# Kernel tables of a state-space layer formed by half chunks of 64 channels instead of quarters of 32

## The chip, the cores and the metric

The kernel runs on one core of a Trainium2 chip. The core has a matrix engine (TensorE, PE in the profile), a vector engine (VectorE, DVE), an engine for functions and casts (ScalarE, ACT), a general engine (GpSimd, POOL) and an engine that mostly issues transfers (SyncE, SP). Each engine runs its instructions in the order in which they stand in its own stream and waits where an operand or a buffer is not ready. The metric is the time of one execution on the device, in microseconds.

## The reference

Two independent layers read their own inputs, and their outputs stand side by side in the result. Part A is attention in which each position sees eight earlier positions, two apart. Part B is a state-space convolution with 640 channels, 192 complex states per channel and 2048 positions:

```python
a: qkv = x @ wqkv                                   # 2048 x 640, 32 heads of 20
   logits = q . k[pos - 2 w] * 20**-0.5, w = 0..7;  attn = softmax;  out = (attn . v) @ wo
b: logdA = dt * (A_re + 1j * A_im)                  # 640 x 192
   P = jnp.exp(logdA[:, :, None] * l[None, None, :])
   K = jnp.einsum("dn,dnl,dn->dl", Cc, P, dB).real  # 640 x 2048, sum over the 192 states
   y = irfft2(rfft2(u, padded) * rfft2(K, padded))[:L] + u * Dskip
```

Nearly all that this document speaks of belongs to K, the sum over 192 states at 2048 positions for 640 channels, and to the Fourier transforms behind it.

## The kernel before, in words

**Chunks, halves, quarters.** The 640 channels are done in five chunks (`NCH = 5`, index `c`) of 128 channels. A chunk has two halves of 64 channels (index `h`), and a half has two quarters of 32 (index `uu`). States lie on partitions. Of a quarter's 32 channels the first 128 states fill all 128 partitions in 32 columns, one a channel; the last 64 states fill 64 partitions, so two channels share each of 16 more columns. The 48 columns are 12 groups `q` of 4 (`f`), and for the sum over states there are matmuls on 128 rows and matmuls on 64.

**Tables.** A power exp(logdA * l) is split into a product of a factor for l's low six bits and one for the rest. The magnitudes come from ACT exponentials (`exps_chunk`, L230 and L232, 45 a chunk, tile `R`). The angles are formed by matmuls into the PSUM tiles `ps_ph` (L257, L260) and turned into sines by ACT (`trig_half`, L264): four tiles `TA` and four tiles `TX` a half. `ps_ph` comes from the pool that also serves the Fourier transforms (tag `bank2`, three buffers).

**Products on DVE.** `small_half` (L280 in the profile, where its helper `TT` is) multiplies the tables of one half: `PG` = magnitude times sine, `Q` = PG times the coefficients `cT`, sums of these into `F` and `G` (both in the tile PG), and per quarter a tile `X` in three operations. `y_form` (L310) then forms, per quarter and for each of k = 0, 1, 2, a tile `Y` from F and G: 12 groups of 64 positions of 4 columns, 3072 elements a partition. Y has the tag `Y` with four buffers, and Q takes one of them.

**Kernel sums on TensorE.** `kgen_unit` (L323 and L328) runs, per quarter and k, 32 matmuls on all 128 partitions and then 32 on 64 partitions, all into one PSUM bank `ps_k` (two buffers). ACT copies that bank into `Ksb` (L329) once a quarter.

**The rest of a chunk.** `coefficients` (L211) makes `cT` for the next chunk by TensorE and four ACT copies. `fwd` transforms (matmuls and casts `A` at L342, L343, then `Sg` at L348, L349), once for K (`transform`) and once for the input u (`fwd_u`). `products` multiplies the two spectra on DVE (`P1`, `P2`, L363). `inverse_a` is the first stage of the inverse transform (matmuls L379, casts `Z` L380). `times_d` (L392) forms the products `UD` of u with the skip weights.

**Order.** The loop over chunks at the end of the program emits, for chunk c: the half-0 products, the transform of chunk c-1, the tables of half 1, the quarter units of half 0 with `products` and `inverse_a` of chunk c-1 between them, `fwd_u`, the half-1 products, the next chunk's coefficients, exponentials and half-0 tables, and the quarter units of half 1. A scheduler then sets each engine's stream by its own estimates; `keep_in_program_order` and `issue_after` pin some instructions to places in it. After the loop stand attention and the second stage of the inverse transform. From 0 to 31 us the program prepares, from 31 to about 298 us it is in the chunk loop, from there to the end in attention and the rest.

Of the kernel before, what the change touches and what calls it, by code (L numbers as in the profile page):

```python
# [10 lines left out]
A = mybir.AluOpType  # L11
# [3 lines left out]
f32 = mybir.dt.float32  # L15
# [79 lines left out]
def partB_prep(tc, pools, prm):  # L95
# [108 lines left out]
    def coefficients(c, pool):  # L204
        for u in range(4):
            sl = slice(32 * u, 32 * u + 32)
            ps = pool.tile([128, 4, UW], f32, name="ps_tr", tag="bank")
            re, im = CN[sl, c, 0], CN[sl, c, 1]
            transposed(u, [(ps[:, 0:4], re, mix[sl, 0:4], True), (ps[:, 1:4], im, mix[sl, 4:7], False),
                           (ps[:, 3:4], re, mix[sl, 7:8], False), (ps[:, 2:3], im, mix[sl, 8:9], False)])  # L210
            nc.scalar.copy(out=cT[:, c, u // 2, :, 12 * (u % 2):12 * (u % 2) + 12, :].rearrange("p w q f -> p w (q f)"), in_=ps[:])  # L211

# [60 lines left out]
def small_half(tc, pools, co, R, TA, TX, h):  # L273

    nc = tc.nc
    V = nc.vector
    tab = pools["tabb"]
    RA, RX = R
    RX = RX[:, 24 * h:24 * h + 24].rearrange("p q (j i) f -> p q j (i f)", j=2)
    TT = lambda o, a, b, op: V.tensor_tensor(out=o, in0=a, in1=b, op=op)  # L280
# [10 lines left out]
    Xs = []  # L291
    for uu in range(2):
        qs = slice(12 * uu, 12 * uu + 12)
        X = tab.tile([128, 12, 3, 32, 4], bf16, name="X", tag="X", bufs=2)
        rows = X[:].rearrange("p q k (j i) f -> p q (k j) (i f)", j=2)
        T = TX[:, qs].rearrange("p q s i f -> p q s (i f)")
        TT(rows[:, :, 0:2], RX[:, qs], bc(T[:, :, 0], 2, 2), A.mult)
        TT(rows[:, :, 2:6:3], RX[:, qs], bc(T[:, :, 1], 2, 2), A.mult)
        TT(rows[:, :, 4:2:-1], rows[:, :, 0:2], rows[:, :, 2:6:3], A.subtract)
        Xs.append(X)  # L300
    return F, G, Xs


def y_form(tc, pools, F, G, uu, k):
    nc = tc.nc
    Y = pools["tabb"].tile([128, 12, 64, 4], bf16, name="Y", tag="Y", bufs=4)
    half = slice(384 * uu, 384 * uu + 384)
    fa = F[:, k, half].rearrange("p (q a f) -> p q a f", a=8, f=4).unsqueeze(2).to_broadcast([128, 12, 8, 8, 4])
    gb = G[:, k, half].rearrange("p (q b f) -> p q b f", b=8, f=4).unsqueeze(3).to_broadcast([128, 12, 8, 8, 4])
    nc.vector.tensor_tensor(out=Y[:].rearrange("p q (b a) f -> p q b a f", a=8), in0=fa, in1=gb, op=A.mult)  # L310
    return Y


def kgen_unit(tc, pools, u, X, Ys, Ksb):

    nc = tc.nc
    MM = nc.tensor.matmul
    ps = pools["psum"].tile([128, 8, 64], f32, name="ps_k", tag="bank", bufs=2)
    for k in range(3):
        for t in range(8):  # L320
            for g in range(4):
                q, f = divmod(8 * g + t, 4)
                MM(ps[32 * g:32 * g + 32, t], lhsT=X[:, q, k, :, f], rhs=Ys[k][:, q, :, f], start=(t == 0 and k == 0), stop=False, tile_position=(0, 32 * g), skip_group_check=True)  # L323
        for t in range(8):
            for g in range(4):
                q, f = divmod(32 + 8 * (g % 2) + t, 4)
                hb = slice(64 * (g // 2), 64 * (g // 2) + 64)
                MM(ps[32 * g:32 * g + 32, t], lhsT=X[hb, q, k, :, f], rhs=Ys[k][hb, q, :, f], start=False, stop=(k == 2), tile_position=(64 * (g // 2), 32 * g), skip_group_check=True)  # L328
    nc.scalar.copy(out=Ksb[:, 8 * u:8 * u + 8, :], in_=ps[:])  # L329

# [77 lines left out]
class Attention:  # L408
# [3 lines left out]

    def __init__(self, tc, pools, A_x, A_wqkv, A_wo, out_a, psk, psg):
# [4 lines left out]
        self.one = lambda name: psg.tile([128, 512], f32, name=name, tag="bank", bufs=2)  # L418
# [39 lines left out]
    def open_first(self, tabb):  # L458

        tile = lambda n, tag, **k: tabb.tile([128, n, 4, 256], bf16, name="prod0", tag=tag, **k)  # L460
        U, K, Y, P = tile(1, "UD"), tile(2, "Ksb"), tile(3, "Y", bufs=4), tile(4, "PG")
        self.first = [[U[:, 0], K[:, 0], Y[:, 0], P[:, 0], P[:, 2]], [Y[:, 2], K[:, 1], Y[:, 1], P[:, 1], P[:, 3]]]
# [229 lines left out]
def body(tc, ctx, pools, prm, B_u, B_Dskip, Sd, Zd, UDd, A_x, A_wqkv, A_wo, out_a, out_b):  # L692
# [14 lines left out]
    with tc.tile_pool(name="prep_l", bufs=1) as pl, tc.tile_pool(name="prep_d", bufs=1) as pd, tc.tile_pool(name="prep_g", bufs=1) as pg, tc.tile_pool(name="prep_h", bufs=1) as ph, tc.tile_pool(name="psum_p", bufs=2, space=bass.MemoryType.PSUM) as psp:  # L707
# [3 lines left out]
        fill(0, 1, lambda u: None)  # L711
        B["coefficients"](0, psp)
        Dn = pl.tile([128, 160], bf16, name="Dn")
# [11 lines left out]
        nc.gpsimd.tensor_copy(out=Dsb[:], in_=Dn[:].rearrange("p (ut c) -> p c ut", c=NCH))  # L725
    psg = ctx.enter_context(tc.tile_pool(name="psum_g", bufs=2, space=bass.MemoryType.PSUM))
    pools["tabb"] = tabs.enter_context(tc.tile_pool(name="tabb", bufs=1, reuse_waits="tile"))
    pools["tabb"].tile([128, LOW], bf16, name="low")
    att = Attention(tc, pools, A_x, A_wqkv, A_wo, out_a, psk, psg)
    Kb, Sk = {}, {}  # L730

    def transform(c):
        Sk[c] = fwd(tc, pools, C, (lambda ut: Kb[c][:, ut, :]), 1, fp)[0]

    def unit(c, h, uu, F, G, X, between=lambda: None):
        Ys = [y_form(tc, pools, F, G, uu, k) for k in range(3)]
        between()
        kgen_unit(tc, dict(pools, psum=psg), 2 * h + uu, X, Ys, Kb[c])
        if 4 * c + 2 * h + uu in UD_AFTER:
            times_d(tc, pools, C, UDd, *divmod(UD_AFTER.index(4 * c + 2 * h + uu), 2))  # L740

# [6 lines left out]

    UD_AFTER = [2, 3, 5, 6, 7, 9, 10, 11, 13, 14]
    LAST = NCH - 1  # L750
    for c in range(NCH):
        Kb[c] = (fp, pools["tabb"])[c % 2].tile([128, 32, 64], bf16, name="Ksb", tag="Ksb")
        F, G, Xs = small_half(tc, pools, B["cT"][:, c], R[c], *trig[c, 0][:2], 0)
# [21 lines left out]
        with ExitStack() as order:  # L775
            if c > 0:
                order.enter_context(tc.issue_after(last.ins))
            F, G, Xs = small_half(tc, pools, B["cT"][:, c], R[c], *trig[c, 1][:2], 1)
# [171 lines left out]
```

## Time and profile before

| | before |
|---|---|
| median of 3 runs | 436.23 us (433.06, 436.23, 437.49) |
| the profiled execution | 432.86 us |
| its span, first to last instruction | 431.1 us |
| mean granted TensorE clock | 0.945 |
| DVE, PE, ACT busy | 379.2, 365.2, 314.1 us |
| Y (60 instructions) | 103.1 us busy, 5.0 us idle ahead of them |
| PG, X waiting for ACT's tables | 7.4 and 3.7 us |
| copies of ps_k (20) | 11.5 us busy, 12.8 us idle ahead of them |

A group's line in the profile reads: line of the program, engine, operation, output <- inputs with partitions and elements per partition, number of instructions, then total busy us and mean ns of one, then the us that the engine stood idle just ahead of these instructions and what ended most of that. Line numbers are those of the program above. A row of 40 digits shows the busy share of each fortieth of the span in tenths. In the timeline a row gives the start in us, the time that a run of equal instructions took, and in brackets the idle time before it.

### The profile page before, as it was taken

To read this page: it belongs to the slowest core of one execution; us is meant where nothing else is said; L and a number is where in the kernel's file an instruction comes from. 1 tells how busy PE (TensorE), PEld (TensorE's weight loads), DVE (VectorE), ACT (ScalarE), POOL (GpSimd) and SP (SyncE) were. 2 spreads that over 40 slices of the span, in tenths; PEclk is the share of its full clock that TensorE was granted. 3 is DMA by queue.
4 is the path that set the end of the run, shared out by engine and by line. 5 is a ranking of instruction groups with operands and counts; after the bars stand their busy time and mean duration, and the time that the engine had idled before them with its cause. 6 is when DMAs were issued, how large, how long until landed. Compare 5 with 4: busy or idle time off the path is not lost.

```text
span 431.1 us, 17929 instructions
## 1 busy us (share of the span) xinstructions
PE 365.2 (85%) x8173; PEld 246.9 (57%) x8173; DVE 379.2 (88%) x353; ACT 314.1 (73%) x574; POOL 39.3 (9%) x83
## 2 busy tenths in 40 slices
PE   1295779989988899888888799999899989879896
PEld 0153566867855678555785567545545666435443
DVE  8899997999966999899996999855978999998751
ACT  3975989889998899979999784433757446546553
POOL 7430000000000000000010000100000300501120
PEclk9998869999895898979999999999999999989999
DMA  5589103082232402334059941700040644888532
GB/s 150 185 158 193 19 2 123 30 268 56 99 149 101 99 28 100 130 120 99 29 200 267 237 117 47 271 2 3 2 99 2 195 89 135 231 202 239 133 95 93
DMA packets 45276, 51.69 MB, mean 120 GB/s; under 512 B 31392, under 2 KB 39136, under 8 KB 42512
## 3 DMA queue, kind: packets, MB, share of 16 engines
q1 hardware_dynamic: 41664, 41.47, 35.8%
q0 software_dynamic: 3392, 8.95, 7.0%
q8 instruction: 64, 1.05, 1.0%
q10 hardware_dynamic: 144, 0.12, 0.1%
q14 instruction: 12, 0.10, 0.1%
HBM read 28.08 MB, written 18.35 MB: 108 GB/s over the span
## 4 chain that ended last, share of the span: by engine, by line
PE 46%; ACT 22%; issue 12%; DVE 9%; DMA 7%; SPq 3%; POOL 1%; DVEq 0%; ACTq 0%; POOLq 0%
PE ps_k L323 7%; PE ps_k L328 7%; ACT A L343 7%; PE ps_ph L257 6%; PE ps_k L476 5%; PE ps_f L348 4%; ACT R L232 4%; PE ps_q L494 4%; PE ps_ph L260 4%; PE ps_op L425 4%; ACT Sg L349 2%; ACT Z L380 2%; DMA LPC<-hi 2%; DVE prod L527 2%; DVE X L280 2%
## 5 line engine op out<-in xcount | busy, mean ns | idle before, releaser
L310 DVE TENSOR_TENSOR Y<-PG 128x3072 bf16<-128x3072 bf16 x60 | 103.1, 1750 | 5.0 <-PE ps_k L328 5.0
L323 PE MATMUL ps_k<-Y,X 128*32 128x64 bf16 x1920 | 47.6, 239 | 7.6 <-issue 4.2
L257 PE MATMUL ps_ph<-LPC 128*128 128x256 bf16 x200 | 41.5, 310 | 14.8 <-DMA LPC<-lo 8.4
L328 PE MATMUL ps_k<-Y,X 64*32 64x64 bf16 x1920 | 45.3, 233 | 4.8 <-issue 4.8
L323 PEld LDWEIGHTS <-X 128*32 128x32 bf16 x1920 | 32.3, 117 | 20.6 <-issue 10.7
L349 ACT CAST Sg<-ps_f 128x1024 bf16<-128x1024 f32 x40 | 37.8, 1033 | 6.5 <-PE ps_f L348 6.3
L232 ACT ACTIVATE R<-LPC 128x192 bf16<-128x192 f32 x155 | 41.4, 372 | 0.0
L280 DVE TENSOR_TENSOR X<-R,TX 128x1536 bf16<-128x1536 bf16 x40 | 37.2, 949 | 3.7 <-ACT TX L264 3.7
L343 ACT CAST A<-ps_f 128x1024 bf16<-128x1024 f32 x40 | 37.7, 1037 | 0.5 <-PE ps_f L342 0.4
L264 ACT ACTIVATE TX<-ps_ph 128x768 bf16<-128x768 int16 x40 | 31.1, 818 | 8.3 <-DVE X L280 3.9
L328 PEld LDWEIGHTS <-X 64*32 64x32 bf16 x1920 | 30.0, 113 | 12.0 <-issue 4.0
L348 PE MATMUL ps_f<-A,T 128*128 128x128 bf16 x320 | 26.2, 249 | 11.6 <-ACT A L343 10.9
L264 ACT ACTIVATE TA<-ps_ph 128x768 bf16<-128x768 int16 x40 | 30.6, 820 | 5.3 <-PE ps_ph L260 5.0
L614 DVE TENSOR_TENSOR prod<-v,atp 128x2048 bf16<-128x2048 bf16 (+2 forms) x32 | 30.8, 1018 | 2.4 <-PE ps_o L425 2.4
L348 PEld LDWEIGHTS <-T 128*128 128x128 bf16 x320 | 23.9, 113 | 12.8 <-issue 11.7
L260 PE MATMUL ps_ph<-LPC 128*64 128x128 bf16 x400 | 29.1, 247 | 0.0
L257 PEld LDWEIGHTS <-LPC 128*128 128x128 bf16 x200 | 14.5, 102 | 23.1 <-DMA LPC<-hi 8.5
L425 PE MATMUL ps_op<-wo,o 128*128 128x320 bf16 x160 | 27.0, 309 | 0.7 <-ACT ob L426 0.4
L260 PEld LDWEIGHTS <-LPC 128*64 128x64 bf16 x400 | 14.9, 116 | 20.2 <-issue 20.1
L363 DVE TENSOR_TENSOR P<-P,Sg 128x4096 bf16<-128x4096 bf16 x10 | 22.8, 2283 | 2.5 <-DMA P<-Sdram 1.5
L426 ACT CAST ob<-ps_op 128x320 bf16<-128x320 f32 x28 | 11.9, 429 | 17.9 <-PE ps_op L425 16.0
L527 DVE TENSOR_TENSOR prod<-qT,kT 128x1024 bf16<-128x1024 bf16 (+1 forms) x16 | 23.0, 1481 | 1.2 <-ACT qT L495 1.2
(132 smaller groups left out, 675.5 us busy)
## 6 DMA issues: line engine op xcount, KB each, us to landing
Sdram<-Sg SPq DMA_DIRECT2D x5, 1024.0 KB
P<-Sdram SPq DMA_DIRECT2D x5, 1024.0 KB
P<-Sdram SPq DMA_DIRECT2D x10, 512.0 KB
Zdram<-Z SPq DMA_DIRECT2D x5, 1024.0 KB
Z<-Zdram SPq DMA_DIRECT2D x30, 128.0 KB
U<-in_B_u_dram SPq DMA_DIRECT2D x4, 640.0 KB
UDdram<-UD SPq DMA_DIRECT2D x10, 256.0 KB
out_dram<-ysb SPq DMA_DIRECT2D x32, 80.0 KB
```

The source lines that it names most:

```text
L232: nc.scalar.activation(out=RX[:, :, e - 16, :], in_=src, func=ACT.Exp, scale=m)
L257: MM(o[:, :, 0:8], lhsT=L[:, 0:128], rhs=rhs, start=first, stop=last, skip_group_check=True)
L260: MM(o[64 * hh:64 * hh + 64, :, 8:12], lhsT=L[:, 128:192], rhs=rhs[:, :, 16 * hh:16 * hh + 16], start=False, stop=last, skip_group_check=T ...
L264: last = nc.scalar.activation(out=dst, in_=words.rearrange("p b (q e f) -> p b q (e f)", e=8, f=4), func=ACT.Sin, scale=PI_LO / 32768.0)
L280: TT = lambda o, a, b, op: V.tensor_tensor(out=o, in0=a, in1=b, op=op)
L310: nc.vector.tensor_tensor(out=Y[:].rearrange("p q (b a) f -> p q b a f", a=8), in0=fa, in1=gb, op=A.mult)
L323: MM(ps[32 * g:32 * g + 32, t], lhsT=X[:, q, k, :, f], rhs=Ys[k][:, q, :, f], start=(t == 0 and k == 0), stop=False, tile_position=(0, 32 ...
L328: MM(ps[32 * g:32 * g + 32, t], lhsT=X[hb, q, k, :, f], rhs=Ys[k][hb, q, :, f], start=False, stop=(k == 2), tile_position=(64 * (g // 2), ...
L343: nc.scalar.copy(out=A1[:, :, 32 * b:32 * b + 32].rearrange("p k (j g) -> p k j g", g=4), in_=ps[:].rearrange("p j k g -> p k j g"))
L348: last = MM(ps[:, kk], lhsT=C["T2"][:, 8 * b + kk, :], rhs=A1[:, 8 * b + kk, :], start=(kk % 4 == 0), stop=True, skip_group_check=True)
L349: nc.scalar.copy(out=Sg[:, :, 8 * b:8 * b + 8, :], in_=ps[:].rearrange("p k (j g) -> p j k g", g=4))
L425: self.MM = lambda *a, **k: self.tc.keep_in_program_order(self.nc.tensor.matmul(*a, **k))
```

## The change

`X` becomes one tile for the 24 groups of a half, in one buffer, formed by three operations of twice the size. `Y` becomes one tile for a half (24 groups, 6144 elements), in two buffers, so in as many bytes as before; Q takes one of the two. `kgen_unit` handles a half: for each k, Y is formed just ahead of its 128 matmuls, the row kinds go 128, 64; 64, 128; 128, 64, and the sum has one PSUM tile of two banks in a pool of its own with one buffer (`psum_n`), copied by ACT once a half. `coefficients` fills one two-bank tile per half from the pool of `ps_ph` and the transforms, so two copies a chunk instead of four. `products` and all of `inverse_a` now stand behind the whole of half 0, and in chunk 0 the input transform `fwd_u(1)` behind the whole of half 1. The first tile of k's halo in attention comes from the shared pool too, and the attention's one-bank pool is opened after the loop.

```diff
     def coefficients(c, pool):
-        for u in range(4):
...
-            ps = pool.tile([128, 4, UW], f32, name="ps_tr", tag="bank")
...
-            nc.scalar.copy(out=cT[:, c, u // 2, :, 12 * (u % 2):12 * (u % 2) + 12, :].rearrange("p w q f -> p w (q f)"), in_=ps[:])
+        for h in range(2):
+            pair = pool.tile([128, 2, 512], f32, name="ps_tr", tag="bank2")
...
+            nc.scalar.copy(out=cT[:, c, h].rearrange("p w (b q) f -> p w b (q f)", b=2), in_=pair.rearrange("p b w x -> p w b x"))
...
-    Q = tab.tile([128, 2, 2, 24, 8, 4], bf16, name="Q", tag="Y", bufs=4)
+    Q = tab.tile([128, 2, 2, 24, 8, 4], bf16, name="Q", tag="Y", bufs=2)
...
-    for uu in range(2):
-        qs = slice(12 * uu, 12 * uu + 12)
-        X = tab.tile([128, 12, 3, 32, 4], bf16, name="X", tag="X", bufs=2)
...
+    X = tab.tile([128, 24, 3, 32, 4], bf16, name="X", tag="X")
+    rows = X[:].rearrange("p q k (j i) f -> p q (k j) (i f)", j=2)
+    T = TX[:].rearrange("p q s i f -> p q s (i f)")
+    TT(rows[:, :, 0:2], RX, bc(T[:, :, 0], 2, 2), A.mult)
+    TT(rows[:, :, 2:6:3], RX, bc(T[:, :, 1], 2, 2), A.mult)
+    TT(rows[:, :, 4:2:-1], rows[:, :, 0:2], rows[:, :, 2:6:3], A.subtract)
...
-    Y = pools["tabb"].tile([128, 12, 64, 4], bf16, name="Y", tag="Y", bufs=4)
+    Y = pools["tabb"].tile([128, 24, 64, 4], bf16, name="Y", tag="Y", bufs=2)
...
-def kgen_unit(tc, pools, u, X, Ys, Ksb):
+def kgen_unit(tc, pools, h, X, Ys, Ksb):
...
-    ps = pools["psum"].tile([128, 8, 64], f32, name="ps_k", tag="bank", bufs=2)
+    ps = pools["psum"].tile([128, 16, 64], f32, name="ps_k", tag="gen")
     for k in range(3):
+        Y = Ys(k)
+        for low in ((0, 1), (1, 0), (0, 1))[k]:
+            first, last = k == 0 and low == 0, k == 2 and low == 1
+            for t in range(16):
+                for g in range(4):
+                    if low:
+                        q, f = divmod(32 + 8 * (g % 2) + t % 8, 4)
+                        rows, at = slice(64 * (g // 2), 64 * (g // 2) + 64), 64 * (g // 2)
+                    else:
+                        q, f = divmod(8 * g + t % 8, 4)
+                        rows, at = slice(0, 128), 0
+                    q += 12 * (t // 8)
+                    MM(ps[32 * g:32 * g + 32, t], lhsT=X[rows, q, k, :, f], rhs=Y[rows, q, :, f], start=(first and t % 8 == 0), stop=last, ...)
-    nc.scalar.copy(out=Ksb[:, 8 * u:8 * u + 8, :], in_=ps[:])
+    nc.scalar.copy(out=Ksb[:, 16 * h:16 * h + 16, :], in_=ps[:])
...
-        ps = self.one("ps_kh")[:, 0:15 * HALO].rearrange("p (c s i) -> p c s i", c=5, s=3)
+        ps = self.big("ps_kh")[:, 0, 0:15 * HALO].rearrange("p (c s i) -> p c s i", c=5, s=3)
...
+    pgen = gen.enter_context(tc.tile_pool(name="psum_n", bufs=1, space=bass.MemoryType.PSUM))
...
-        unit(c, 0, 0, F, G, Xs[0])
+        unit(c, 0, F, G, X)
         if c > 0:
             P1, P2, last = products(tc, pools, Sk[c - 1], Sd[c - 1], fp, True)
             ia = inverse_a(tc, pools, C, P1, P2, Zd[c - 1], fp)
-            ia[0]()
-        unit(c, 0, 1, F, G, Xs[1])
-        if c > 0:
-            for f in ia[1:]:
+            for f in ia:
                 f()
...
-                B["coefficients"](c + 1, psg)
+                B["coefficients"](c + 1, psk)
...
-            unit(c, 1, 0, F, G, Xs[0])
+            unit(c, 1, F, G, X, q_first if c == LAST else lambda: None)
         if c == 0:
             fwd_u(tc, pools, C, Sd, 1)
-        unit(c, 1, 1, F, G, Xs[1], q_first if c == LAST else lambda: None)
...
+    gen.close()
+    att.psg = ctx.enter_context(tc.tile_pool(name="psum_g", bufs=2, space=bass.MemoryType.PSUM))
```

More of the change, by code (lines that the diff above doesn't have):

```diff
@@ L310, in y_form @@
     nc.vector.tensor_tensor(out=Y[:].rearrange("p q (b a) f -> p q b a f", a=8), in0=fa, in1=gb, op=A.mult)
     return Y
-def kgen_unit(tc, pools, u, X, Ys, Ksb):
+def kgen_unit(tc, pools, h, X, Ys, Ksb):
     nc = tc.nc
     MM = nc.tensor.matmul
-    ps = pools["psum"].tile([128, 8, 64], f32, name="ps_k", tag="bank", bufs=2)
+    ps = pools["psum"].tile([128, 16, 64], f32, name="ps_k", tag="gen")
     for k in range(3):
[L320 to L328, printed above, removed]
-    nc.scalar.copy(out=Ksb[:, 8 * u:8 * u + 8, :], in_=ps[:])
+        Y = Ys(k)
[10 more added lines that the diff above has]
+                    q += 12 * (t // 8)
+                    MM(ps[32 * g:32 * g + 32, t], lhsT=X[rows, q, k, :, f], rhs=Y[rows, q, :, f], start=(first and t % 8 == 0), stop=last, tile_position=(at, 32 * g), skip_group_check=True)
+    nc.scalar.copy(out=Ksb[:, 16 * h:16 * h + 16, :], in_=ps[:])
@@ L408, with __init__ @@
 class Attention:
-    def __init__(self, tc, pools, A_x, A_wqkv, A_wo, out_a, psk, psg):
+    def __init__(self, tc, pools, A_x, A_wqkv, A_wo, out_a, psk):
         self.tc, self.nc, self.ta, self.ident = tc, tc.nc, pools["bbase"], pools["ident"]
@@ L417, in __init__ @@
         self.big = lambda name: psk.tile([128, 2, 512], f32, name=name, tag="bank2")
-        self.one = lambda name: psg.tile([128, 512], f32, name=name, tag="bank", bufs=2)
+        self.one = lambda name: self.psg.tile([128, 512], f32, name=name, tag="bank", bufs=2)
         self.lsb, self.at, self.obs = {}, {}, {}
@@ L460, in open_first @@
         tile = lambda n, tag, **k: tabb.tile([128, n, 4, 256], bf16, name="prod0", tag=tag, **k)
-        U, K, Y, P = tile(1, "UD"), tile(2, "Ksb"), tile(3, "Y", bufs=4), tile(4, "PG")
+        U, K, Y, P = tile(1, "UD"), tile(2, "Ksb"), tile(3, "Y", bufs=2), tile(4, "PG")
         self.first = [[U[:, 0], K[:, 0], Y[:, 0], P[:, 0], P[:, 2]], [Y[:, 2], K[:, 1], Y[:, 1], P[:, 1], P[:, 3]]]
@@ L711, in body @@
         fill(0, 1, lambda u: None)
-        B["coefficients"](0, psp)
+        B["coefficients"](0, psk)
         Dn = pl.tile([128, 160], bf16, name="Dn")
@@ L747, in q_first @@
                 att.first_products(w, ct)
-    UD_AFTER = [2, 3, 5, 6, 7, 9, 10, 11, 13, 14]
-    LAST = NCH - 1
     for c in range(NCH):
         Kb[c] = (fp, pools["tabb"])[c % 2].tile([128, 32, 64], bf16, name="Ksb", tag="Ksb")
-        F, G, Xs = small_half(tc, pools, B["cT"][:, c], R[c], *trig[c, 0][:2], 0)
+        F, G, X = small_half(tc, pools, B["cT"][:, c], R[c], *trig[c, 0][:2], 0)
         if c > 0:
```

51 lines of the change are left out of this document (26 added, 25 removed).

## The prediction

> **What bounds the kernel now.** I read the busy shares first, then the stages, then who waits for whom on the busiest engine, then the one place where the change adds a wait. The page's first part and its 40 slices:
>
> ```profile
> PE 365.2 (85%) x8173; PEld 246.9 (57%) x8173; DVE 379.2 (88%) x353; ACT 314.1 (73%) x574; POOL 39.3 (9%) x83
> ...
> PE   1295779989988899888888799999899989879896
> ...
> DVE  8899997999966999899996999855978999998751
> ```
>
> Three engines are nearly full, VectorE (DVE) most. The chunk loop runs from about 31 to 298 us. Cut by chunks (columns: window, length, busy us of TensorE, weight load, DVE, ScalarE (ACT) and GpSimd, granted clock, share of the DMA engines, GB/s):
>
> ```profile
> 133.00:184.00 51.00, 45.06 (x1053) 34.43 (x1049) 48.91 (x40) 47.55 (x91) 0.62 (x2) 0.87 0.25 81
> 184.00:236.00 52.00, 44.55 (x1184) 33.23 (x1181) 47.73 (x38) 47.97 (x92) 1.77 (x2) 0.95 0.48 137
> ```
>
> In a chunk of 51 us DVE is busy 48.9 and ACT 47.6: a middle chunk is a relay between two engines without slack, and TensorE has some 6 us of it. What DVE waits for (total us, times, longest):
>
> ```profile
> DVE PG L280 <- ACT TA L264: 7.4, 2, 5.7
> ...
> DVE Y L310 <- PE ps_k L328: 5.0, 5, 2.2
> DVE X L280 <- ACT TX L264: 3.7, 1, 3.7
> ```
>
> Sixteen us in the loop. Y is the operation that the change resizes; its 5.0 us are waits for a Y buffer that TensorE still reads. The groups:
>
> ```profile
> L310 DVE TENSOR_TENSOR Y<-PG 128x3072 bf16<-128x3072 bf16 x60 | 103.1, 1750 | 5.0 <-PE ps_k L328 5.0
> L323 PE MATMUL ps_k<-Y,X 128*32 128x64 bf16 x1920 | 47.6, 239 | 7.6 <-issue 4.2
> L280 DVE TENSOR_TENSOR X<-R,TX 128x1536 bf16<-128x1536 bf16 x40 | 37.2, 949 | 3.7 <-ACT TX L264 3.7
> ```
>
> **1. Fewer, larger DVE instructions: -4.2 us.** 60 Y of 3072 elements become 30 of 6144, and 60 X operations of 1536 become 30 of 3072: 60 instructions fewer, the same elements. What one costs beyond its elements is read from instructions that follow each other:
>
> ```profile
> 43.16 8.42 DVE L310 TENSOR_TENSOR Y<-PG 128x3072 bf16<-128x3072 bf16 x5
> ```
>
> Five Ys in 8.42 us, the last alone 1.75: one every (8.42 - 1.75)/4 = 1.67 us. X operations of 1536 follow each other every 0.87 (36.68 to 37.55, say). So 0.80 us per 1536 elements, a fixed 0.07, and 3.26 for a Y of 6144. 60 x 0.07 = 4.2. DVE is full in these stages, so I count it whole. The single durations would have a fixed part of 2 x 949 - 1750 = 148 ns, but the pitch says that neighbours overlap by half of it; I go by the pitch, since these operations follow each other. The Trainium skill, "VectorE: DVE Perf Modes", section "Side-by-side: where the cycles go for N=2048 bf16", has about 150 cycles of init and decode at 0.96 GHz in every instruction; by it 60 fewer would give an estimated 9.4 us and the sum would end 5 lower. The single durations agree with it, the pitch does not.
>
> **2. ACT: about 2.5 us less work, not on its own a gain.** 20 copies of ps_k at 582 ns (L329) become 10 of 1024 elements; the A casts of that size take 1037. That is 11.5 - 10.4 = 1.1. The 20 coefficient copies at 344 become 10 of 384 elements: by the slope of those two casts, 0.45/512 us per element, about 0.51 each, 1.7 less. It helps only where ACT is late; I count it in step 4.
>
> **3. TensorE: fewer switches, nothing on the path.** The matmuls are the same 3840. Today runs of 32 of one row kind alternate, about 0.60 each (starts at 177.10, 177.71 and 178.29), 12 runs a half, 7.2 us. The changed order has runs of 64 and 128 and 3 changes of kind instead of 11. Within a run a group of four comes about every 0.06, eight of them 0.48, so a change costs some 0.12 and eight fewer are worth 1 us a half, 10 in all. TensorE has idle time in these stages, and what decides is when a part of it can start: 0 counted; bounds -10 and 0.
>
> **4. The new wait: the third Y of each half, +18 us.** Before, four Y slots of a quarter: five Ys can stand ahead of the matmuls by four, in steps of 1.67 us. After, two slots of double size: same bytes, but a slot is given back only when all 128 matmuls of a k are done. Q takes one of the slots, then Y0 and Y1 are formed, and Y2 waits for the whole of k=0. So DVE stops until TensorE is through k=0, and queued behind Y2 stand the UD product, P1 and P2 (half 0) or the next half's PG, for which ia, Z and the next matmuls wait.
>
> When is it through? In the built program the scheduler has set the k=0 matmuls of a half among the ps_ph matmuls of the next trig tables, and ps_ph has three buffers: its n-th tile waits for the (n-3)rd sine of ACT. In chunks 2 and 3, half 1, the 128th matmul of k=0 stands behind the sixth ps_ph, so behind the third sine. Those sines stand on ACT behind Z, A, Sg, coefficients, exponentials and a table load. Today's durations (chunk 2):
>
> ```profile
> 165.68 3.78 ACT L343 CAST A<-ps_f 128x1024 bf16<-128x1024 f32 x4
> ...
> 170.56 3.79 ACT L349 CAST Sg<-ps_f 128x1024 bf16<-128x1024 f32 x4
> ...
> 174.45 4.43 ACT L232 ACTIVATE R<-LPC 128x192 bf16<-128x192 f32 x17
> 178.90 1.28 ACT L264 ACT_TABLE_LOAD   x1
> 180.19 2.22 ACT L264 ACTIVATE TA<-ps_ph 128x768 bf16<-128x768 int16 x3
> ```
>
> Set in the changed order from the end of P2, which releases both sides. ACT: the ia matmuls come every 0.061 us, so its second piece is there at 1.6; 4 Z and 4 A casts at 0.91 reach 8.9; eight ps_f matmuls 0.7, four Sg 3.8: 13.4; two coefficient copies 1.0: 14.4; the 7 exponentials that are left behind them, 0.25 each: 16.1; table load 1.28: 17.4; three sines 2.2: 19.6; then the sixth ps_ph and 14 to 20 ps_k matmuls, 1.3: TensorE ends k=0 at 20.9. DVE: PG, X, Q at 1.67; 0.47, 0.87; X 1.67; 0.47; X 1.67; Y0 and Y1 at 3.26: ready for Y2 at 16.7. **Y2 waits 4.2 us**, in chunk 2 and in chunk 3.
>
> The same count elsewhere: chunk 0 half 1, where seven ps_ph and a whole block of exponentials stand ahead, 4 to 5.5; chunk 1 half 0, behind A casts and the fifth sine, 4.4 to 5; the other half of chunk 1 (265 matmuls ahead of the fourth ps_ph) and the halves 0 of chunks 2 to 4 and half 1 of 4, where only three Ys' worth of TensorE time (2.2 us a k against 3.26 of Y1) is asked, 0.4 to 2 each, 6 together. Sum 8.4 + 4.8 + 4.7 + 6 = 24, against 5.0 now. I take 23: **+18**. Bounds: below, today's longest such wait, 2.2, at the four large places and half of the 6 elsewhere, 12 (+7); above, 5.5 at the four and 2 at each of the others, 34 (+29).
>
> **5. What falls away.** When Y2 has waited, the work after it is late and finds its tables ready: the 3.7 (X at 236.45, the start of chunk 4) and the 1.71 (PG at 183.94, the start of chunk 3) are such, and the 5.65 (PG at 132.72) shrinks to one or two: **-6.5**, bounds -9 to -3. ACT's 2.5 us are in it.
>
> **6. The order behind it: +3.** ps_k has one buffer and one copy a half, so the second copy waits for all 384 matmuls, and the A casts queue behind it on ACT; P1 and P2, today between the Ys of a half, stand behind all of them and UD, and with them ia and Z. A copy of Ksb waits 0.64 us today (12.8 over 20); one a chunk is 3. Bounds 0 to 15 (a whole Y, 3 us, a chunk). The coefficients' move into the three-buffer pool ps_ph uses costs its copies' time, which is in step 4. The Y bytes, the DMAs and the attention (298 to 431 us) are the same: 0; k_halo's one tile in the other pool is hidden by the ps_k2 casts.
>
> **Sum.** -4.2 + 18 - 6.5 + 3 = **+10.3** on the profiled execution, 432.9 us (span 431.1): 443. That execution lies 3.4 under the median, 436.2; on the median it is 446.5. I say 445.
>
> **Rivals.**
> *The DVE ledger alone, faster.* If TensorE reaches the end of k=0 before DVE asks for its slot (the sines' chain under 16.7 us from P2), no third Y waits: -4.2 - 5.0, 0 to 4 back at step 6: 424 to 428. For it: TensorE has slack and larger runs; ACT gets lighter. Against: the 26 us from P2 (155.9) to the third sine's end (182.4) today.
> *Half-sized waits, no change.* ACT's chain is shorter than I set it and the waits are half my count (14 in all): +9 - 4.2 - 6.5 + 1.5, nothing: 433 to 440.
> *Worse.* The copy of 1024 and the late P2 each push ACT's chain, and each chunk's period adds another 2 us: +20, 452 to 460.
> *The fixed part in full.* If the larger instructions save the whole 148 ns each, 60 x 0.148 = 8.9 instead of 4.2, and the rest stands: 445 - 5 = 440. Against it: the pitch of 1.67. (It is what the Trainium skill's page named in step 1 would make of it.)
>
> **Chances.** The forecast, slower by 5 to 16 us, 0.63; ledger alone 0.13; half-sized waits 0.10; worse 0.09; the fixed part in full 0.05, which is within 1% as the half-sized waits are. Range 433 to 456: it leaves out the ledger case and half of the worse one. A kernel within 1% (4.4 us) can't be told from no change: faster 0.13, same 0.15, slower 0.72.
>
> **What would show it.** Y x30 with about 3.33 us each and 20 us or more of idle ahead of it, released by PE ps_k (step 4); under 8 us there falsifies it. Step 1: the DVE's busy time of PG, X and Y lower by 4 to 9. Step 3: ps_k groups shorter, their idle longer. Step 5: PG and X waiting less for TA, TX. Step 6: longer waits of L329's copy, P2 later in each chunk. Wrong it would be if the scheduler's ps_ph find their sines done earlier than my ACT chain, or if the attention moves too.

## The result: slower by 3.6%

| | before | changed |
|---|---|---|
| median of the runs beside each other | 436.24 us (433.06 to 437.49) | 455.18 us (447.65 to 456.47) |
| ratio to before | | 1.0356 (95% interval 1.0273 to 1.0439) |
| the profiled execution, its span | 432.86, 431.1 us | 456.34, 454.6 us |

The ratio leaves the longest runs out, so it is smaller than the quotient of the medians; by it the change costs 15.5 us, where the prediction's sum has 10.3. The median, 455.18 us, lies just inside the stated range of 433 to 456, and also inside the 452 to 460 of the rival named worse. The profiled execution of the changed kernel is one of its longer ones, so sums over it explain 23.5 us.

What bounds the engines, from the page of the changed kernel:

```profile
PE 359.5 (79%) x8173; PEld 249.4 (55%) x8173; DVE 376.2 (83%) x293; ACT 312.6 (69%) x554; POOL 39.1 (9%) x83
...
L308 DVE TENSOR_TENSOR Y<-PG 128x6144 bf16<-128x6144 bf16 x30 | 100.2, 3358 | 31.0 <-PE ps_k L330 31.0
L330 PE MATMUL ps_k<-Y,X 128*32 128x64 bf16 (+1 forms) x3840 | 76.0, 238 | 23.4 <-issue 12.3
```

All four engines are less busy than before, and the program is longer: time went into waiting. What DVE waited for (total us, times, longest):

```profile
DVE Y L308 <- PE ps_k L330: 31.0, 9, 5.8
...
DVE P L365 <- DMA P<-Sdram: 5.3, 3, 2.5
DVE atp L616 <- PE ps_o L427: 4.9, 2, 3.5
DVE X L283 <- DMA LPC<-hi: 4.6, 1, 4.6
```

Against the page before, Y's wait grew by 26.0, P's loads by 3.8, the attention's atp by 3.7, and a wait of 4.6 ahead of the first X is new; the waits for TA and TX fell from 11.1 to 0.7, and DVE is busy 3.1 less. Together +24.6, against the 23.5 by which the span grew; smaller differences make up the rest.

So far it looks like the forecast come true: a third Y that waits. In chunk 2 the forecast's own example can be laid beside the trace (start, length, operation, idle time before it):

```profile
180.88 6.61 DVE L308 TENSOR_TENSOR Y<-PG 128x6144 bf16<-128x6144 bf16 x2
193.28 3.36 DVE L308 TENSOR_TENSOR Y<-PG 128x6144 bf16<-128x6144 bf16 x1 [5.79 <-PE ps_k L330]
```

P2 ends at 170.80. DVE is ready for the third Y at 187.49, 16.7 us later, as forecast. ACT is 1.1 us later than forecast at A and at the third sine, TensorE ends k=0 22.5 us after P2 instead of 20.9, and the wait is 5.79 us instead of 4.2. Whether this wait is the cause of the loss is what the experiments are about.

### The profile page after: what moved, and what is told of

The parts are those of the page before. It is cut to its first block, busy times and chain, and to the rows that moved or that the text cites. A ratio compares the mean times of both kernels' runs of the same rounds, so it can differ in the third digit from the quotient of the medians.

```text
span 454.6 us, 17834 instructions
## 1 busy us (share of the span) xinstructions
PE 359.5 (79%) x8173; PEld 249.4 (55%) x8173; DVE 376.2 (83%) x293; ACT 312.6 (69%) x554; POOL 39.1 (9%) x83
## 4 chain that ended last, share of the span: by engine, by line
PE 44%; DVE 18%; ACT 13%; issue 11%; DMA 7%; SPq 6%; DVEq 0%; ACTq 0%
PE ps_k L330 9%; ACT A L345 6%; DVE Y L308 5%; PE ps_ia L381 5%; PE ps_k L478 5%; PE ps_ph L260 5%; PE ps_op L427 5%; PE ps_q L496 4%; PE ps_ph L263 3%; DVE P L365 3%; ACT Sg L351 3%; DVE X L283 2%; PE ps_f L350 2%; PE ps_o L427 2%; SPq L672 2%
## 5 line engine op out<-in xcount | busy, mean ns | idle before, releaser
L308 DVE TENSOR_TENSOR Y<-PG 128x6144 bf16<-128x6144 bf16 x30 | 100.2, 3358 | 31.0 <-PE ps_k L330 31.0
L330 PE MATMUL ps_k<-Y,X 128*32 128x64 bf16 (+1 forms) x3840 | 76.0, 238 | 23.4 <-issue 12.3
L330 PEld LDWEIGHTS <-X 128*32 128x32 bf16 (+1 forms) x3840 | 60.6, 115 | 35.2 <-issue 27.3
L260 PE MATMUL ps_ph<-LPC 128*128 128x256 bf16 x200 | 40.2, 311 | 10.4 <-ACT TX L267 9.5
L283 DVE TENSOR_TENSOR X<-R,TX 128x3072 bf16<-128x3072 bf16 x20 | 35.0, 1758 | 4.6 <-DMA LPC<-hi 4.6
L350 PE MATMUL ps_f<-A,T 128*128 128x128 bf16 x320 | 23.5, 232 | 15.9 <-ACT A L345 14.2
L381 PE MATMUL ps_ia<-EA,P 128*128 128x128 bf16 x320 | 27.3, 263 | 7.6 <-DVE P L365 7.6
L381 PEld LDWEIGHTS <-P 128*128 128x128 bf16 x320 | 25.7, 122 | 9.7 <-DVE P L365 8.7
L350 PEld LDWEIGHTS <-T 128*128 128x128 bf16 x320 | 21.0, 104 | 17.8 <-issue 17.1
L263 PE MATMUL ps_ph<-LPC 128*64 128x128 bf16 x400 | 28.6, 251 | 0.0
L331 ACT CAST Ksb<-ps_k 128x1024 bf16<-128x1024 f32 x10 | 10.0, 1003 | 26.7 <-PE ps_k L330 26.7
L260 PEld LDWEIGHTS <-LPC 128*128 128x128 bf16 x200 | 15.6, 105 | 19.5 <-issue 11.4
L263 PEld LDWEIGHTS <-LPC 128*64 128x64 bf16 x400 | 15.5, 121 | 18.7 <-issue 18.7
```

Of the source, the lines that this page charges most:

```text
L260: MM(o[:, :, 0:8], lhsT=L[:, 0:128], rhs=rhs, start=first, stop=last, skip_group_check=True)
L263: MM(o[64 * hh:64 * hh + 64, :, 8:12], lhsT=L[:, 128:192], rhs=rhs[:, :, 16 * hh:16 * hh + 16], start=False, stop=last, skip_group_check=T ...
L330: MM(ps[32 * g:32 * g + 32, t], lhsT=X[rows, q, k, :, f], rhs=Y[rows, q, :, f], start=(first and t % 8 == 0), stop=last, tile_position=(at ...
L350: last = MM(ps[:, kk], lhsT=C["T2"][:, 8 * b + kk, :], rhs=A1[:, 8 * b + kk, :], start=(kk % 4 == 0), stop=True, skip_group_check=True)
L381: MM(ps[:, j], lhsT=P[:, 8 * b + j].rearrange("p k g -> p (k g)"), rhs=C["EA"][:, w, :], start=(j % 4 == 0 and w == 0), stop=(w == 1), ski ...
```

## Experiments

All ratios are to the kernel before, run beside each other; 0.01 is 4.36 us. "Chunk 1" and so on below is the stretch from the PG of half 1 of the chunk before to the PG of half 1 of this chunk.

**Y back to quarters, k outermost.**

```diff
-    Y = pools["tabb"].tile([128, 24, 64, 4], bf16, name="Y", tag="Y", bufs=2)
+    Y = pools["tabb"].tile([128, 12, 64, 4], bf16, name="Y", tag="Y", bufs=4)
...
-        for low in ((0, 1), (1, 0), (0, 1))[k]:
-            for t in range(16):
+        for v, low in [(v, low) for v in range(2) for low in (0, 1)]:
+            for t in range(8 * v, 8 * v + 8):
```

> The changed kernel with Y alone put back to quarters: 12 groups, 3072 elements, four buffers, the same bytes; X, the sum's tile, the coefficients, and the places of P1 and P2 stay changed, and k stays the outer loop (quarter 0 then quarter 1 of each k). A slot now comes back after 64 matmuls instead of 128, and in chunks 2 and 3, half 1, those 64 stand ahead of the fourth ps_ph in the built order. Theory (what a slot holds sets the wait): the waits of Y for PE ps_k fall from 31.0 to 5 to 12 us, no wait of 4 us or more in chunks 2 and 3; 30 more Y cost 2.1 us; some 5 us come back as waits for TA and TX; ratio to before 1.00 to 1.015. Rival (TensorE and ACT are late whatever the slot holds): what Y no longer waits, PG and X wait for TA and TX, and the ratio stays at 1.03 to 1.04.

Measured: 1.0251 (1.0166 to 1.0335), Y's waits 18.6 us, longest 5.0. Neither: the waits fell by 12 us, the time by some 4 to 5, within the two intervals, and the waits for TA did not come back. Half a slot is not enough to end the wait. By stages it is clearer: chunks 2 to 4, where Y waits 11.6 us instead of 19.3, took 158.3 us instead of 165.7 (159.1 before), and chunk 1 stayed long, 56.9 us against 50.6 before. The edit also puts the row kinds back to one change every 32 matmuls, which the expectation does not count.

**k=0 pinned ahead of ps_ph.**

```diff
+            if k0 is not None and (kind, uu) == (0, 1):
+                order.enter_context(tc.issue_after(k0.ins))     # third and fourth ps_ph
...
+        half = unit(c, 1, F, G, X, ...); k0 = next(half)         # Y0 and the 128 matmuls of k=0 first
-        trig[c + 1, 0] = trig_half(tc, pools, B, c + 1, 0)
+        trig[c + 1, 0] = trig_half(tc, pools, B, c + 1, 0, k0)
```

> The changed kernel, buffers untouched, with the 128 matmuls of k=0 of a half pinned ahead of the ps_ph matmuls that wait for sines. Theory (the sines on ACT hold the matmuls that give the slot back): the waits of Y for PE ps_k fall from 31.0 to 3 to 10 us; the sines come a little later, so that PG and X wait 5 to 11 us for TA and TX, as before; ratio 1.00 to 1.02. Rival (k=0 is late for a reason of its own, the 2.2 us of its matmuls behind Y0 and TensorE's other work): the waits stay above 20 us and the ratio at 1.03 to 1.04.

Measured: 1.0322 (1.0266 to 1.0378), Y's waits 15.5 us. The sum hides two opposite effects. Chunks 2 to 4 took 155.9 us, against 165.7 in the changed kernel and 159.1 before; chunk 1 took 62.7 against 57.9 and 50.6. The reason stands in the run with both edits, below.

**X's buffer laid ahead of Y's.**

```diff
+    X = tab.tile([128, 24, 3, 32, 4], bf16, name="X", tag="X")
     Q = tab.tile([128, 2, 2, 24, 8, 4], bf16, name="Q", tag="Y", bufs=2)
...
-    X = tab.tile([128, 24, 3, 32, 4], bf16, name="X", tag="X")
```

> The changed kernel with X's buffer laid ahead of the two Y buffers in the pool, so at other addresses; the order of instructions on every engine is the same. The trace of the changed kernel has one wait of 4.58 us ahead of the first X, released by a transfer out of a preparation tile. Theory (X, now one tile for the whole half, lies over a preparation tile that a transfer still reads, where before only the second quarter's X did and came 6 us later): the wait goes, chunk 0 is 3 to 4.6 us shorter, ratio 1.025 to 1.03. Rival (the first X waits for ACT's TX, which the trace puts down to the transfer): the wait stays and the ratio is 1.036.

Measured: 1.0268 (1.0208 to 1.0329). The first X follows PG without a wait, and half 0 of chunk 0 takes 20.1 us instead of 24.8 (21.2 before). The timeline of DVE in this run, and the same place in the changed kernel:

```profile
31.43 1.75 DVE L283 TENSOR_TENSOR PG<-R,TA 128x3072 bf16<-128x3072 bf16 x1
33.09 1.75 DVE L283 TENSOR_TENSOR X<-R,TX 128x3072 bf16<-128x3072 bf16 x1
```

```profile
38.64 1.76 DVE L283 TENSOR_TENSOR X<-R,TX 128x3072 bf16<-128x3072 bf16 x1 [4.58 <-DMA LPC<-hi]
```

The order of instructions is the same in both, so the wait is one for memory: the larger X lay over a preparation tile that a transfer still read. The trace shows it gone; of the time, 3.8 us, the intervals overlap.

**Both edits.** The same two, in one kernel.

> Both: k=0 pinned ahead of ps_ph, and X's buffer laid ahead of Y's. Theory: the two add up, ratio 0.99 to 1.01; Y's waits as with the pin alone, no wait ahead of the first X. Rival (the time lost is elsewhere: one buffer for the sum, its one copy, P1 and P2 behind a whole half): ratio 1.02 or more although Y hardly waits.

Measured: 1.0280 (1.0192 to 1.0368), outside the theory's range, with 16.8 us of waits left ahead of Y. Whether the two add up cannot be said: by the single runs the sum would be 1.023, inside the interval. Chunk 1 took 63.4 us. ACT's timeline shows where:

```profile
34.38 1.51 ACT L271 ACTIVATE TA<-ps_ph 128x768 bf16<-128x768 int16 x2 [1.07 <-PE ps_ph L266]
48.49 1.51 ACT L271 ACTIVATE TA<-ps_ph 128x768 bf16<-128x768 int16 x2 [12.60 <-PE ps_ph L266]
```

In half 0 of chunk 0 the pin put the sines of half 1 behind k=0, which was not there before 47 us; ACT stood idle for 12.6 us. Whether this is what lengthens chunk 1, the next run tests.

**The pin not in half 0 of chunk 0.**

```diff
-        trig[c, 1] = trig_half(tc, pools, B, c, 1, next(half))
+        k0 = next(half) if c > 0 else None
+        trig[c, 1] = trig_half(tc, pools, B, c, 1, k0)
```

> As the run with both (k=0 pinned ahead of ps_ph, X's buffer laid first), but half 0 of chunk 0 is not pinned. There the pin set the sines of chunk 0 half 1 behind k=0 and ACT stood idle for 12.6 us, and chunk 1 (from its predecessor's second PG to its own) took 63.4 us instead of 50.6 before and 59.5 without the pin. Chunks 2 to 4 together took 157.9 us against 159.1 before and 164.9 without the pin. Theory: chunk 1 falls to 53 to 57 us, chunks 2 to 4 stay at 157 to 159, ratio 1.005 to 1.015. Rival (chunk 1 is long for the late P loads and the transform behind the half, whatever the sines): it stays above 60 and the ratio at 1.025 or more.

Measured: 1.0154 (1.0078 to 1.0230), chunk 1 55.3 us, chunks 2 to 4 158.0: the theory's numbers, just above the upper end of its ratio.

**The coefficients' matmuls behind k=0 too.**

```diff
+            k0 = next(half)
+        if c < LAST:
             with tc.issue_after(trig[c, 1][2].ins):
+                with tc.issue_after(k0.ins):
+                    B["coefficients"](c + 1, psk)
```

> As the run before it, and in every half 1 the coefficients' matmuls (now in the pool of three buffers that the transforms and ps_ph use) also stand behind k=0. In half 1 of chunk 0 they stood inside k=0 and waited there for the buffers of Sg. Theory (a second thing that holds k=0): Y's waits for PE ps_k fall to 3 to 9 us, the wait in half 1 of chunk 0 from 6.2 to under 2, chunk 1 another 2 to 4 us shorter, ratio 0.995 to 1.01. Rival (ACT's chain sets the end of that half, DVE waits for TA instead): ratio within 0.005 of the run before it.

Measured: 1.0102 (1.0021 to 1.0183). Y hardly waits; the waits for TA are back:

```profile
DVE PG L287 <- ACT TA L271: 9.6, 3, 6.0
...
DVE Y L312 <- PE ps_k L334: 4.8, 2, 2.9
DVE UD L400 <- DMA UDdram<-UD: 4.6, 3, 2.1
DVE P L371 <- issue: 3.4, 1, 3.4
```

The part this run adds is not shown to be a gain: the ratio fell by 0.0052, within the intervals, chunk 1 took 55.3 us as in the run before it instead of 2 to 4 less, and chunks 2 to 4 took 159.3 against 158.0. DVE now waits for TA, as the rival says.

With TensorE's order alone the change goes from 1.027 to 1.010, with two large slots as they were. Y's waits fell by 27.8 us for it (32.6 to 4.8), the time by 7.2. But it does not reach 1, with 60 DVE instructions fewer. So I took the change apart from the other end.

**One sum a half, alone on the kernel before.**

```diff
-    ps = pools["psum"].tile([128, 8, 64], f32, name="ps_k", tag="bank", bufs=2)
+            halfsum[0] = pgen.tile([128, 16, 64], f32, name="ps_k", tag="gen")      # once a half
...
+    if u % 2 == 1:
+        nc.scalar.copy(out=Ksb[:, 8 * u - 8:8 * u + 8, :], in_=pair[:])
```

with the coefficients in pairs and k's halo from the shared pool, as in the change.

> The kernel before, with Y, X and the order of the units untouched, and only these parts of the change: the sums of a half in one tile of two banks with one buffer, copied once a half; the coefficients in pairs from the shared pool; k's halo from it. It prices step 6 of the prediction by itself. By the prediction, +3 (0 to 15) us less 2.5 of ACT: ratio 0.995 to 1.02, and the copies' idle time grows from 12.8 us to 20 or more. Rival (this part is the larger one, since the transforms' casts queue behind the half's copy): ratio 1.025 or more.

Measured: 1.0126 (1.0052 to 1.0199), inside the forecast of that part. The copies' idle time fell, to 8.4 us, against the expectation; it is Y, still in quarters, that waits 12.2 us instead of 5.0. With one buffer TensorE cannot begin a half's sum before the copy of the last; that this is the reason was not tested.

**X for a half, alone on the kernel before** (laid ahead of Y).

```diff
-    for uu in range(2):
-        X = tab.tile([128, 12, 3, 32, 4], bf16, name="X", tag="X", bufs=2)
+    X = tab.tile([128, 24, 3, 32, 4], bf16, name="X", tag="X")
```

> The kernel before, and only X changed: one tile for a half in one buffer, three operations instead of six, its buffer laid ahead of Y's so that the wait at the start is out of the way. It prices half of step 1: 30 instructions of 0.07 us fewer, -2.1 us, and single buffering of X, which may add waits for PE ps_k ahead of X. Ratio 0.99 to 1.005 by the prediction. Rival (X in one buffer is a new wait of its own): X waits 5 us or more for ps_k and the ratio is 1.01 or more.

Measured: 0.9892 (0.9841 to 0.9943), 432.09 us against 435.12. By the ratio this part of the change is a gain of 4.7 us (2.5 to 6.9); the medians of all runs differ by 3.0. The rival's wait is there too (X, in one buffer, waits 9.4 us for ps_k), while Y's waits went from 5.0 to 1.3 and those for TA and TX from 11.1 to 5.1. These waits are from an execution of 436.28 us, one of the kernel's longer ones and longer than the one profiled before, so the trace does not show where the gain comes from.

**The order alone, on the kernel before.** No tile and no size is touched.

```diff
         unit(c, 0, 0, F, G, Xs[0])
+        unit(c, 0, 1, F, G, Xs[1])
         if c > 0:
             P1, P2, last = products(tc, pools, Sk[c - 1], Sd[c - 1], fp, True)
             ia = inverse_a(tc, pools, C, P1, P2, Zd[c - 1], fp)
-            ia[0]()
-        unit(c, 0, 1, F, G, Xs[1])
-        if c > 0:
-            for f in ia[1:]:
+            for f in ia:
                 f()
...
+        unit(c, 1, 1, F, G, Xs[1], ...)
         if c == 0:
             fwd_u(tc, pools, C, Sd, 1)
-        unit(c, 1, 1, F, G, Xs[1], ...)
```

> The kernel before with tiles, buffers and sizes untouched, and only the order of the change: P1, P2 and all of ia behind the whole of half 0, and in chunk 0 the transform of u for chunk 1 behind the whole of half 1. The other half of step 6. Measured so far as ratios to before: the change 1.036, its sum's tile and coefficients alone 1.013, X alone (at the good address) 0.989, X's address 0.009; 0.025 is left for Y's two large slots and for this order. Theory (Y's slots are most of it): 0.998 to 1.010, and P waits for its loads less than 4 us. Rival (the late P and the late transform are most of it): 1.015 or more.

Measured: 1.0305 (1.0252 to 1.0358). My theory fell: moving P1, P2, ia and one transform behind the Ys makes the kernel as slow as the whole change, and Y, in quarters with four slots, waits 17.8 us. Where P1 and P2 stand in chunk 2, in the kernel before:

```profile
144.75 3.42 DVE L310 TENSOR_TENSOR Y<-PG 128x3072 bf16<-128x3072 bf16 x2
148.09 2.28 DVE L363 TENSOR_TENSOR P<-P,Sg 128x4096 bf16<-128x4096 bf16 x1
150.29 3.42 DVE L310 TENSOR_TENSOR Y<-PG 128x3072 bf16<-128x3072 bf16 x2
153.63 2.28 DVE L363 TENSOR_TENSOR P<-P,Sg 128x4096 bf16<-128x4096 bf16 x1
155.83 1.75 DVE L310 TENSOR_TENSOR Y<-PG 128x3072 bf16<-128x3072 bf16 x1
157.50 1.31 DVE L392 TENSOR_TENSOR UD<-U,Dsb 128x1024 bf16<-128x1024 bf16 x1
158.75 1.74 DVE L280 TENSOR_TENSOR PG<-R,TA 128x3072 bf16<-128x3072 bf16 x1
```

and with the order alone changed:

```profile
161.30 3.43 DVE L310 TENSOR_TENSOR Y<-PG 128x3072 bf16<-128x3072 bf16 x2 [2.54 <-PE ps_k L328]
164.65 1.33 DVE L392 TENSOR_TENSOR UD<-U,Dsb 128x1024 bf16<-128x1024 bf16 x1
165.89 4.49 DVE L363 TENSOR_TENSOR P<-P,Sg 128x4096 bf16<-128x4096 bf16 x2
170.29 1.75 DVE L280 TENSOR_TENSOR PG<-R,TA 128x3072 bf16<-128x3072 bf16 x1
```

Before, three Ys and UD stand behind P1, and one Y and UD behind P2; now nothing does. Chunks 2 to 4 took 169.9 us, 10.8 more than before, and in them Y waits 14.9 us instead of 1.2: the order makes the wait of step 4 in small slots, too.

**Y back to quarters in the order of before, quarter outermost,** on the change with X laid first.

```diff
-    for k in range(3):
-        Y = Ys(k)
+    for v in range(2):
+        Yk = Ys(v)                     # three Ys of one quarter, four slots
```

> The changed kernel with X's buffer laid first (1.027 by itself) and with Y put back to quarters in four slots and in the order of before, so that a quarter's three k follow each other; all else stays changed, the order of P1, P2 and the transform too. Only Y's slots and their order are undone. Theory (Y's slots): Y's waits for PE ps_k 32.6 to 15 us or less, ratio 1.000 to 1.012. Rival (the order of the transforms and products): ratio 1.018 or more.

Measured: 1.0261 (1.0199 to 1.0323), against 1.0268 with the two large slots: the difference is 0.0007, and by the two intervals it is known to about 0.009, or 4 us. Y's waits fell from 32.6 to 17.8 us, near what was expected, and the ratio did not follow. That is not yet a proof that the large slots are free. The edit puts back 30 Ys (2.1 us by step 1) and the changes of row kind (ps_k busy 10.3 us longer) along with the small slots. And in the two profiled executions chunks 2 to 4, with 11.4 us of Y's waits instead of 19.7, took 158.6 us instead of 164.9, and the whole span is 5.1 us shorter.

**X for a half and the alternating rows,** on the kernel before.

```diff
     for k in range(3):
-        for t in range(8):                                 # 128 rows
...
-        for t in range(8):                                 # 64 rows
...
+        for low in ((0, 1), (1, 0), (0, 1))[k]:
+            for t in range(8):                             # 64 rows if low, else 128
```

> The kernel before with X as one tile for a half (0.989 by itself) and, of the change, also the alternating row kinds of the matmuls (128, 64; 64, 128; 128, 64), so 3 changes of kind a unit instead of 5; the order on every engine stays. Step 3 counted this at 0: ratio 0.985 to 0.993, ps_k's busy time up to 5 us lower. Rival (TensorE's time is on the path): 0.98 or lower.

Measured: 0.9978 (0.9940 to 1.0016). The ps_k matmuls, time in which they overlap counted once, are busy 3.8 us less than with X alone, as expected, and the ratio is outside the range given. It is 0.9% above that of X alone, but by the medians of all runs (432.89 against 434.65, and 432.09 against 435.12) the two are 0.996 and 0.993. The twelve runs went from 426 to 440 us, and the profiled one is the shortest of them. Whether the alternating rows cost anything is open; a gain is not shown.

**The order put back in the change** (X laid first, large Ys and one sum kept).

```diff
-        unit(c, 0, F, G, X)
+        half = unit(c, 0, F, G, X); next(half)          # up to the matmuls of k=1
         if c > 0:
             P1, P2, last = products(...); ia = inverse_a(...)
+            ia[0]()
+        for _ in half: pass                              # Y2, k=2, the copy, UD
+        if c > 0:
-            for f in ia:
+            for f in ia[1:]:
                 f()
```

and in chunk 0 the transform for chunk 1 ahead of k=2 in the same way.

> The changed kernel with its large tiles and its one sum kept, X's buffer laid first (1.027 by itself), and the order put back as far as halves allow: P1, P2 and the first piece of ia between the matmuls of k=1 and those of k=2 of half 0, the other pieces behind the half, and in chunk 0 the transform for chunk 1 ahead of k=2 of half 1. The order alone, laid on the kernel before, made it 1.031. Theory now (the late P2, and with it ia, Z and the sines behind them on ACT, is most of the loss; the waits of Y are where DVE shows it): ratio 0.995 to 1.010 with Y's two large slots untouched, Y's waits for PE ps_k 20 us or less. Rival (the loss of the large slots is a cause of its own of the same size): ratio 1.018 or more, Y's waits still near 30 us.

Measured: 1.0116 (1.0072 to 1.0159) against 1.0268 without: 6.6 us back, with the large slots untouched and Y still waiting 21.1 us. It is between the two, a little above the theory's range. The run tests the order within itself, too. Only in chunk 2 did the scheduler set both products ahead of the third Y:

```profile
149.16 3.36 DVE L308 TENSOR_TENSOR Y<-PG 128x6144 bf16<-128x6144 bf16 x1
152.43 4.50 DVE L367 TENSOR_TENSOR P<-P,Sg 128x4096 bf16<-128x4096 bf16 x2
156.83 3.36 DVE L308 TENSOR_TENSOR Y<-PG 128x6144 bf16<-128x6144 bf16 x1
```

There the stretch from PG to the end of P2 took 22.4 us (23.2 before, 29.0 in the change); in chunks 1, 3 and 4, with P2 behind the third Y, 29.5, 26.8 and 28.6. Part of the gain went again: from that P2 to the next PG it took 29.7 us, 27.0 in the change.

## Why the prediction was right, and where its reasons were wrong

**What the loss is.** A chunk is a ring of two stretches. From the end of P2 ACT is the longer part: Z, A, Sg, exponentials, sines, up to the next PG of half 0. From that PG to the end of P2, DVE is, and the next Z waits for it. Means of chunks 2 to 4, from the timeline of DVE:

| | end of P2 to PG | PG to end of P2 | ring | ratio |
|---|---|---|---|---|
| before | 29.5 us | 22.7 us | 52.2 us | 1 |
| changed | 26.9 | 28.3 | 55.3 | 1.036 |
| order alone, on before | 27.8 | 28.8 | 56.6 | 1.031 |
| change, X's buffer first | 26.9 | 28.1 | 55.0 | 1.027 |
| the same, Y in quarters | 25.4 | 27.5 | 52.9 | 1.026 |
| the same, k=0 pinned, not in half 0 of chunk 0 | 27.0 | 25.7 | 52.7 | 1.015 |
| change with X first and the order put back | 26.8 | 25.9 | 52.8 | 1.012 |
| X for a half, on before | 28.1 | 23.9 | 52.0 | 0.989 |

Before, a Y or two and a UD stood behind P2 and lay beside ACT's chain, where DVE had to wait for the sines anyway (5.65, 1.71 and 3.71 us). The order of the change puts them ahead of P2, into the stretch that ACT's next chain waits for: 5.6 us longer a chunk, 2.6 of them given back in the other stretch. Of the 5.6, the Ys and UD that stood behind P2 are 3.0 (2.8, 4.5 and 1.6 in chunks 2, 3 and 4), and waits of the third Y and of P's loads in this stretch 1.9; with the order alone, the waits of Y there are 3.2 of 6.1. That the order costs 13.3 us on the kernel before was shown by laying it on alone; that it does so through these Ys and UD is read from the rings, not tested.

The ring is not the whole loss. Of the 23.5 us between the two profiled executions, 12.0 are there when P2 of chunk 1 ends (115.1 us against 103.1), 9.2 come in the three rings, and 2.3 after them. And the ring comes back to between 52 and 53.1 us in three ways: by the order put back, by Y in quarters, and by k=0 pinned. This points to the late P2, the large slot and the late k=0 acting together in chunks 2 to 4, none of them the cause alone; it rests on one profiled execution of each run. The runs with Y in quarters and with the pin still lose 1.0 to 3.2%, much of it in chunk 1, which takes 55.3 to 63.4 us in them and 50.6 before, and up to 6.5 us behind the loop. Apart from the pin in chunk 0, what lengthens chunk 1 was not taken apart.

**Step 1** (-4.2, the fixed part of a DVE instruction): DVE is 3.1 us less busy, and the groups of Y and X are 5.1 less, inside the 4 to 9 named as a sign. Three large Ys in 9.89 us come every (9.89 - 3.36)/2 = 3.27 us, as worked out (3.26):

```profile
47.13 9.89 DVE L308 TENSOR_TENSOR Y<-PG 128x6144 bf16<-128x6144 bf16 x3
```

The Trainium skill, "Vector Engine (DVE) Microarchitecture Reference", section "5.2 Measured stream behaviour on trn2 (trn3 not measured)", gives about 75 ns for an instruction after queue overlap, measured on 32-bit streams; the 0.07 agrees with it. The 150 cycles weighed in the prediction fit the single durations only. The rival with the fixed part in full, 8.9 us, falls with DVE's 3.1.

**Step 2** (ACT 2.5 less): 1.5 less; the copies of ps_k took 1003 ns and those of the coefficients 510, against 1037 and 510 worked out.

**Step 3** (fewer changes of row kind, 10 us of TensorE, 0 on the path): it came as worked out. The two lines of ps_k before, 47.6 and 45.3 us, overlap in time, so their sum is not to be set against the one line of 76.0 after. With overlapping time counted once, all matmuls into tiles named ps_k (100 of the attention included) are busy 108.8 us before and 98.6 after: 10.3 less, 0.13 for each of 80 changes. The idle time ahead of them rose from 12.4 to 23.4, and no gain of time from it could be seen. The Trainium skill, "TensorEngine Tiling (Array Packing)", section "Key Properties", says that a change of tiling mode drains TensorE; the price of a change is in keeping with that, though no run here isolates a drain.

**Step 4** (the third Y, +18) had the wait right and its price wrong. The mechanism was there to the detail: 31.0 us of waits for 23, in the four places named (5.79 and 5.84 for 4.2 in chunks 2 and 3, 4.40 and 4.71 in chunk 0 half 1 and chunk 1 half 0), and in a fifth, chunk 1 half 1, 4.74 where at most 2 were counted. But a microsecond of this wait is not a microsecond of time, as step 4 has it. With k=0 and the coefficients pinned on TensorE, 27.8 us fewer of them gave 7.2 us, and DVE waited for TA instead. Y in quarters took away 14.8 us (32.6 to 17.8) and 0.3 us of time by the ratios, known to about 4, or 5.1 by the two profiled executions. And the order alone makes such waits with small slots, so they are not the slots' alone. The waits show where DVE stands in a loop that is too long. What the size of the slots costs by itself stays open: the two runs with Y in quarters give 7.4 and 6.4 us back in chunks 2 to 4 of their profiled executions, and less over the whole.

**Step 5** (-6.5): the waits for TA and TX fell by 10.4, more than the bound of 9. It is the same ring seen from its other side.

**Step 6** (+3, bounds 0 to 15): mis-sized. It named the late P1, P2, ia and Z, and priced them by the idle time ahead of a copy. On the kernel before, the order alone is +13.3 us and the one sum with its coefficients +5.5; either is above the +3. Their sum, 18.8, was not measured and need not hold: in chunks 2 to 4 they add 10.8 and 4.4 us alone, while the change with X first and Y in quarters, which has both, takes 0.5 us less there than the kernel before.

**Counted at 0:** the first X waits 4.6 us at its new address, and without it half 0 of chunk 0 is 4.7 us shorter and the ratio 3.8 us lower, with overlapping intervals; P's loads 3.8 more.

So the direction was foreseen for a good reason, a third Y that waits for k=0, and that the size came within 5 us is in part luck: the price of step 4 was too high and that of step 6 too low, and the two are entangled. The measured parts (order +3.05%, one sum +1.26, X's address +0.9, X -1.1) add up to 4.1% against 3.6 for the change, without anything for Y; but the sum is known only to about 1.5 points and the change to 0.8, so some 5 us for Y cannot be excluded. Of the rivals, the DVE ledger alone and the half-sized waits are refuted by the 31.0 us. The case named worse, at 0.09, a late P2 that lengthens each chunk's period (by 3.1 us here), was near on the period and on the median.

**What stays open:** the two repairs, TensorE's order and the place of P1 and P2, were not tried together, and neither with X alone. Large slots with the rest of the kernel before were not tried, nor small slots in the change with its row order kept. The best version by the ratio is X for a half on the kernel before, 0.989.

## What to carry to other kernels

In a loop where two engines hand work to each other, measure the ring from hand-over to hand-over and ask of every moved instruction on which side of the hand-over it now stands; the same work can be hidden on one side and lengthen the loop on the other. The largest new wait in a profile shows where the late engine stands, not what it costs: undo what it is put down to, and see whether the time follows, stage by stage and over the whole. Parts measured alone need not add up. When lines of a profile are added, ask whether their times overlap. A merged tile is also a tile at other addresses, and its first use may have to wait for whatever lay there.

## What the runs showed of the hardware that was not expected

Fewer changes of row kind took work off TensorE, 10.3 us of ps_k in the change and 3.8 in the run with alternating rows, and no gain of time from it could be seen in either. One kernel's own runs spread by 13 us (427.2 to 440.2 for X alone, ten runs), so that of two edits near 0.99 only many runs can tell the better.
